# Attention values of two pairs of head groups: column tiles with a transpose by DMA in place of token-wise matmuls

## The chip, the cores and the metric

The kernel runs on one core of a Trainium2 chip. The metric is the device time of one execution in microseconds, lower is better; several executions are timed and the median is given. One further execution was recorded by the hardware profiler: its span runs from the first to the last instruction, and its own time, with what lies around the span, stands beside it in the table below.

## The reference: what is computed

Two layers follow each other twice: an attention with a compressive memory, and a feed-forward net with ReLU. The input has 2048 tokens of 640 features, all in bf16; there are 32 heads of 20 features, and the tokens are cut into 4 segments of 512.

```python
x = x + _A_ref(_layernorm(x), wq, wk, wv, wo, beta)
x = x + _B_ref(_layernorm(x), w1, w2)      # 640 -> 1728 -> 640
# ... and both once more

# _A_ref, for each segment s of 4 (q, k, v by head: [32, 512, 20])
logits = einsum('bhqd,bhkd->bhqk', qs, ks) * scale + mask   # causal in the segment
p      = softmax(logits)
a_dot  = einsum('bhqk,bhkd->bhqd', p, vs)
num    = einsum('bhld,bhde->bhle', phi(qs), M)
den    = einsum('bhld,bhd->bhl', phi(qs), z) + 1e-6
o      = g * num / den + (1 - g) * a_dot                    # g = sigmoid(beta)
M, z   = M + phi(ks)^T vs, z + sum(phi(ks))
# at the end: concat(o) @ wo
```

The change is about `a_dot`: the product of the softmax's numerators with the values, and the division by their sum.

## The kernel before

**A planner.** The kernel writes no fixed order. `plan` describes the work as some thirty streams (generators), each yielding operations (`Op`) with an engine, an assumed duration and what they wait for. `Sched.run` repeatedly takes the operation that can start first, with priorities (0 is the highest) as the tie-breaker, and so lays down each engine's order and its semaphore waits before anything runs. Slots (`Slot`, `Acq`) stand for buffers: PSUM banks, staging tiles, the padded queries and keys. Events (`S.set`, `Need`) link the streams. `dma` puts all transfers in this part of the program on SP's queue, which is worked off in order; `turn` (line 668) is a DMA that transposes 128x128 blocks, and the planner takes SP as held while it is under way.

The whole plan is made once for each price of a mode change of TensorE in `STARTS` (line 161), and the plan whose end in the planner's model, summed over four draws of random DMA delays (`late`), is the lowest is emitted (line 1534). TensorE is used in three modes, `full`, `rows` (scores: four row tiles, for four heads of 20 features) and `cols` (column tiles). An operation in `cols` is put off by up to `JOIN_NS` = 4 us if the array is in full mode, so that it can stand behind a set of scores. Where the planner sees TensorE idle for long, `keep_busy` puts in multiplications of the identity matrix that nothing uses (line 627).

**Attention.** The 32 heads form 8 groups of four. Two groups make a pair, and pairs are numbered by `m`: 0 to 3 for segment 0 of the first layer, 4 to 7 for segment 1, and so on to 31. For each pair:

- `scores` (line 1082) multiplies keys by queries, one set for each of five rounds; PSUM banks 0 and 1 (X) and 2 and 3 (Y) hold it.
- `exps` (line 1137) takes the exponential on ACT, 128x1024 elements at a time, into the buffer PT (two slots, one for each group of the pair); `causal` (line 1161) zeroes what lies above the diagonal on GpSimd.
- `apply` (line 1227) multiplies by the values, each of which has a 1 as its 21st element (`VAUG`), so that the row's sum comes out beside the product. When a group's matmuls are done, its PT slot is free for the next pair.

`apply` has two ways. *By tokens* (`values_by_token`, line 1181): PT is the stationary operand, 128 keys by 128 queries, and 21 columns of values are streamed, 40 matmuls for a group (4 heads x 10 blocks on or below the diagonal). The result has tokens on partitions, so DVE divides straight from PSUM into `o_sb` with three instructions for a group (lines 1209, 1210, 1213). *By column tiles* (lines 1236 to 1259): the values of one head, 21 to 32 columns wide, are the stationary operand in a quarter of the array, and PT is streamed, 16 matmuls for a group, the four heads of a block in four column tiles. The result has features on partitions. It is copied out of PSUM to `av` by DVE or ACT (`evac`, lines 1254 and 1255), both groups of the pair are transposed by one DMA to `avt` (`turn_av`, line 1263), and `divide` (line 1271) takes the reciprocal, multiplies by 1 - g, and writes `o_sb` with one instruction for each group (lines 1282, 1283, 1290). `av` and `avt` are single slots. The stream of `divide` has priority 6, that of `apply` 1, that of `turn_av` 2.

Pairs 0 to 3 (segment 0 of the first layer) go by tokens, pairs 4 to 31 by column tiles.

**Around it.** When all of a segment's `o_sb` is there, `turn_o` (line 1323) transposes it in two DMAs to `oT`, `out_proj` (line 1335) multiplies by wo, the result is added to x (line 1317), normalized (`ln_b`) and transposed again, and `ffn` follows. For segment 0 of the first layer these steps are marked as urgent (`HOT`). In the meantime TensorE does what lies ahead: queries, keys and values of the following segments (lines 640 and 643), and updates of the memory (line 1047). Queries and keys go to DRAM and come back in padded form (`spill` line 889, `fill` line 934), the latter's loads on SP's queue; phi(k) is transposed by a DMA (`turn_k`).

Of the kernel before, what the change touches and what calls it, by code (L numbers as in the profile page):

```python
# [14 lines left out]
NSEG = 4  # L15
# [4 lines left out]
G = H // 4  # L20
# [137 lines left out]

LONE_NS = 300.0
SWITCH_NS = 97.0  # L160
STARTS = [SWITCH_NS + 0.75 * (k - 32 // 2) for k in range(32)]
LATE_NS = 300.0
JOIN_NS = 4000.0
SEM_NS = 60.0
# [212 lines left out]
def pe(ns, fns, waits=(), acq=None, take=(), mode="full"):  # L377
    return Op([("pe", ns, fns, 190.0)], waits, acq=acq, take=take, mode=mode)
# [14 lines left out]
def evac(n, mode, vfn, afn, waits=(), psum=True):  # L393
    return Op([("act", (52.0 if psum else 94.0) + n / 1.2, [(afn, True)], 125.0),
               ("dve", 66.0 + n / (0.96 * mode), [(vfn, True)], 95.0)], waits, urgent=True)
# [12 lines left out]
def plan(switch, sb, sem_, psum, dram, A_x, A_wq, A_wk, A_wv, A_wo, A_beta, B_x, B_w1, B_w2, out):  # L408
# [435 lines left out]
    def vx(a, s):  # L844

        return 3 if (a, s) == (0, 0) else (NSEG * a + s) % 3
# [328 lines left out]
    def wide(g, hh):  # L1175

        return 32 if (g, hh) != (G - 1, 3) else DH + 1

    BY_TOKEN = ((0, 0),)

    def values_by_token(m, a, s, g0, vt):

# [37 lines left out]
    def done_values(a, s, g0, tk):  # L1220
        if g0 == G - 2:
            dmt = yield Need("dm", a, s)
            VA[vx(a, s)].release(tk, *dmt)
            if (a, s) == (0, 0):
                S.set("v00", tks=VA[3].tks)

    def apply(m):

        a, r = divmod(2 * m, NSEG * G)
        s, g0 = divmod(r, G)  # L1230
        vt = yield Need("v", a, s)
        if (a, s) in BY_TOKEN:
            tk = yield from values_by_token(m, a, s, g0, vt)
            yield from done_values(a, s, g0, tk)
            return
        sl = None
        ev = []
        for z in range(2):
            mk = yield Need("p", 2 * m + z)
            pt, mk = mk[0], mk[1:]  # L1240
            if sl is None:
                sl = yield Acq([AV])
            fns = []
            for j in range(NJ):
                for hh in range(4):
                    fns.append((lambda e, bk, j=j, hh=hh, pt=pt, g=g0 + z: e.matmul(  # L1246
                        bk.ap[32 * hh:32 * hh + wide(g, hh), 128 * j:L],
                        VAUG[vx(a, s)][:, j].rearrange("p h e -> p (h e)")[
                            :, (4 * g + hh) * (DH + 1):(4 * g + hh) * (DH + 1) + wide(g, hh)],
                        pt.ap[:, hh, PT_OFF[j]:PT_OFF[j] + L - 128 * j], start=(j == 0), stop=(j == NJ - 1)),  # L1250
                        j == NJ - 1 and hh == 3))
            bk, tk = yield pe(545.0, fns, mk + vt, acq=MISC, mode="cols")
            pt.release(tk)
            te = yield evac(L, 1, lambda e, sl=sl, z=z, bk=bk: e.tensor_copy(sl.ap[:, z], bk.ap),  # L1254
                            lambda e, sl=sl, z=z, bk=bk: e.activation(sl.ap[:, z], bk.ap, ACT.Copy), [tk] + sl.tks)
            bk.release(te)
            ev.append(te)
        S.set("av", m, tks=[sl] + ev)
        yield from done_values(a, s, g0, tk)

    LATER = range(len(BY_TOKEN) * G // 2, NSEG * G)

    def turn_av(m):
        ev = yield Need("av", m)
# [185 lines left out]
    def hot(f):  # L1450

        def g(a, s):
            if (a, s) not in HOT:
                yield from f(a, s)
                return
            gen = f(a, s)
            y = next(gen, None)
            while y is not None:
                if isinstance(y, Op):
                    y.urgent = 0.8  # L1460
                r = yield y
                try:
                    y = gen.send(r)
                except StopIteration:
                    return
        return g
# [5 lines left out]
    def each(f):  # L1472
        for a, s in AS:
            yield from f(a, s)

    def items(f, count):
        for n in (range(count) if isinstance(count, int) else count):
            yield from f(n)

    S.add(0, scores())  # L1480
    S.add(0, exps())
    S.add(5.5, items(causal, NSEG * G))
    S.add(1, items(apply, NSEG * G))
    S.add(2, items(turn_av, LATER))
    S.add(6, items(divide, LATER))
    S.add(2, each(hot(turn_o)))
# [31 lines left out]
def bass_interleave_layers__memory_aug_infini_attn__dense_activation_relu__prompt_kernel(  # L1518
    nc, A_x, A_wq, A_wk, A_wv, A_wo, A_beta, B_x, B_w1, B_w2, out,
):  # L1520
    with contextlib.ExitStack() as es:
        kept = {}

        def once(name, make):
            if name not in kept:
                kept[name] = make()
            return kept[name]

        sb = lambda name, shape, dtype=dt.bfloat16: once(name, lambda: es.enter_context(nc.sbuf_tensor(name, shape, dtype)))
        sem_ = lambda name: once("s_" + name, lambda: es.enter_context(nc.semaphore(name)))  # L1530
        psum = lambda name, shape: once(name, lambda: es.enter_context(nc.psum_tensor(name, shape, dt.float32)))
        dram = lambda name, shape: once(name, lambda: nc.dram_tensor(name, shape, dt.bfloat16, kind="Internal").ap())
        plans = [plan(k, sb, sem_, psum, dram, A_x, A_wq, A_wk, A_wv, A_wo, A_beta, B_x, B_w1, B_w2, out) for k in STARTS]
        S = min(plans, key=lambda p: sum(p.late(n) for n in range(4)))
        with nc.Block() as block:
            S.P.emit(block)
    return S
# [28 lines left out]
```

## Time and profile before

| what | value |
|---|---|
| three executions | 564.82, 566.28, 566.39 us |
| median | 566.28 us |
| profiled execution: time | 565.3 us |
| profiled execution: span | 563.5 us |
| matmuls by tokens (line 1197) | 320, that is 8 groups of 40 |
| matmuls by column tiles (line 1246) | 896, that is 56 groups of 16 |
| sets of 128x1024 exponentials (line 1155) | 320, mean 1022 ns |
| TensorE clock granted, mean | 1.000 |

A row of the profile's order of time gives the start and the length in microseconds, the engine (PE is TensorE, SPq the queue of SyncE), the line of the kernel, the operation, what it writes and reads, and how many like ones were merged; in square brackets stands the idle time of the engine just before, and what ended it. Matmuls are pipelined: the length of a row of several includes the drain of the last, so the time that a group holds the array is read from its start to the start of the next row. A row of the groups by line has the count, the busy time in us with the mean length of one in ns, and the idle time before them with what ended it. A row of the stages has, for each engine, its busy time and its number of instructions, then the granted clock, the DMA engines' busy share and GB/s.

### The profile page before, as it was taken

The page shows a single profiled execution, that of the slowest core. Times are in us where ns is not written, and L with a number is a line of the kernel's source. Part 1 is how long each engine was busy: PE and PEld are TensorE (multiplying, and loading weights), DVE is VectorE, ACT ScalarE, POOL GpSimd, SP SyncE. Part 2 cuts the span into 40 slices and gives each one's busy share as a digit, 9 for nine tenths or more (in the row PEclk, how much of TensorE's full clock was granted, in tenths as well). Part 3 has the DMA queues.
Part 4 walks back from the last instruction along what each step waited for, and adds up shares of the span by engine and source line. Part 5 has one row for each costly group of instructions (what it writes and reads, how often), then busy time and mean ns, then how long its engine had stood idle before and what let it go on. Part 6 is the DMA issues. An engine that isn't in the chain of part 4 may idle for free.

```text
span 563.5 us, 12875 instructions
## 1 busy us (share of the span) xinstructions
PE 556.4 (99%) x5219; PEld 305.0 (54%) x5219; DVE 420.1 (75%) x1070; ACT 404.2 (72%) x512; POOL 195.1 (35%) x302
## 2 busy tenths in 40 slices
PE   8999999999999999999999999999999999999998
PEld 7664555445554454645446544555445654665655
DVE  6989789888999689878898997688747964560202
ACT  4789998987788878778986688778878678113140
POOL 4544344333344335444433443035322433110000
PEclk9999999999999999999999999999999999999999
DMA  8695988383474136542375131880326410512101
GB/s 268 120 221 138 238 218 182 74 224 56 97 171 94 44 88 159 118 95 72 92 163 115 27 66 26 193 148 20 67 80 173 109 43 20 116 45 48 47 1 47
DMA packets 130109, 60.93 MB, mean 108 GB/s; under 512 B 108930, under 2 KB 119938, under 8 KB 130050
## 3 DMA queue, kind: packets, MB, share of 16 engines
q1 hardware_dynamic: 129830, 59.85, 45.5%
q8 instruction: 41, 0.67, 0.5%
q10 hardware_dynamic: 220, 0.26, 0.2%
q14 instruction: 18, 0.15, 0.1%
HBM read 20.57 MB, written 12.85 MB: 59 GB/s over the span
## 4 chain that ended last, share of the span: by engine, by line
PE 87%; DVE 8%; DMA 2%; ACT 1%; SPq 1%; issue 0%
PE ps L643 56%; PE ps L640 11%; PE ps L1103 8%; PE ps L1246 6%; DVE stats L651 2%; PE ps L996 2%; PE ps L1197 1%; PE ps L1047 1%; DVE x_sb L1317 1%; PE ps L1394 1%; DMA avt<-av 1%; DVE xn_tok L705 1%; SPq L913 1%; DMA oT<-o_sb 1%; ACT PT L1155 1%; DVE stg L816 1%
## 5 line engine op out<-in xcount | busy, mean ns | idle before, releaser
L1155 ACT ACTIVATE PT<-ps 128x1024 bf16<-128x1024 f32 x320 | 310.0, 1022 | 70.3 <-PE ps L1103 64.6
L1167 POOL TENSOR_SCALAR_AFFINE_SELECT PT<-PT 128x512 bf16<-128x512 bf16 x256 | 166.6, 668 | 268.2 <-ACT PT L1155 267.9
L643 PE MATMUL ps<-w_r,hT 128*128 128x320 bf16 (+2 forms) x768 | 123.0, 299 | 0.0
L643 PE MATMUL ps<-xnT,w_r 128*128 128x512 bf16 x416 | 113.3, 379 | 0.0
L1317 DVE TENSOR_TENSOR x_sb<-x_sb,ps 128x320 bf16<-128x320 bf16 (+1 forms) x128 | 60.3, 479 | 66.7 <-PE ps L643 66.0
L643 PEld LDWEIGHTS ps<-w_r,hT 128*128 128x128 bf16 x768 | 72.4, 98 | 31.9 <-issue 4.4
L1425 ACT ACTIVATE hT<-ps 128x512 bf16<-128x512 f32 x55 | 32.7, 598 | 50.0 <-PE ps L643 49.7
L1103 PE MATMUL ps<-pad 20*128 20x128 bf16 (+3 forms) x1024 | 64.8, 301 | 1.6 <-ACT PT L1155 0.9
L643 PEld LDWEIGHTS ps<-xnT,w_r 128*128 128x128 bf16 x416 | 39.7, 98 | 44.0 <-issue 3.2
L651 DVE BATCH_NORM_STATS2 stats<-x_sb 128x6 f32<-128x320 bf16 x126 | 56.4, 472 | 2.1 <-DMA x_sb<-in_A_x_dram 1.8
L1254 DVE CAST av<-ps 128x512 bf16<-128x512 f32 x53 | 36.2, 684 | 14.8 <-PE ps L1246 14.7
L1103 PEld LDWEIGHTS ps<-pad 20*128 20x128 bf16 x1024 | 18.3, 92 | 52.6 <-ACT PT L1155 25.6
L643 PE MATMUL ps<-wo_r,oT 128*128 128x320 bf16 x256 | 46.1, 299 | 0.0
L1246 PE MATMUL ps<-PT,v_aug 128*32 128x256 bf16 (+5 forms) x896 | 40.7, 302 | 0.0
L1423 DVE TENSOR_SCALAR hT<-ps 128x512 bf16<-128x512 f32 x49 | 33.4, 683 | 9.1 <-PE ps L643 9.0
L640 PE MATMUL ps<-xnT,w_r 128*128 128x512 bf16 x104 | 39.6, 380 | 0.0
L643 PE MATMUL ps<-wv_r,xnT 128*128 128x320 bf16 x192 | 36.7, 300 | 0.0
L643 PE MATMUL ps<-xnT,wk_r 128*128 128x512 bf16 (+1 forms) x140 | 36.1, 349 | 0.0
L643 PE MATMUL ps<-xnT,wq_r 128*128 128x512 bf16 (+1 forms) x140 | 34.9, 349 | 0.0
L665 POOL TENSOR_TENSOR rstd<-lnU,mhalf 128x2 f32<-128x2 f32 (+2 forms) x25 | 20.8, 831 | 38.0 <-DVE lnU L661 34.4
L816 DVE CAST stg<-ps 128x512 bf16<-128x512 f32 (+1 forms) x48 | 29.5, 618 | 3.3 <-PE ps L643 3.2
L1290 DVE TENSOR_TENSOR o_sb<-avt,rden 128x320 bf16<-128x320 bf16 x56 | 30.5, 562 | 0.6
(117 smaller groups left out, 695.8 us busy)
## 6 DMA issues: line engine op xcount, KB each, us to landing
pad<-scr SPq DMA_DIRECT2D x124, 80.0 KB
scr<-stg SPq DMA_DIRECT2D x34, 256.0 KB, 2.9
out_dram<-x_sb SPq DMA_DIRECT2D x15, 160.0 KB, 1.8
w_r<-in_B_w_dram SPq DMA_DIRECT2D x10, 216.0 KB, 4.2
w_r<-in_B_w_dram SPq DMA_DIRECT2D x13, 160.0 KB, 2.8
x_sb<-in_A_x_dram SPq DMA_DIRECT2D x9, 160.0 KB, 2.8
scr<-w_r SPq DMA_DIRECT2D x5, 256.0 KB, 3.6
x_sb<-in_A_x_dram SPq DMA_DIRECT2D x3, 320.0 KB, 7.2
```

What stands on the lines that cost most here:

```text
L640: bk, tk = yield pe(mm_ns(n), [(lambda e, bk, a=a, b=b: e.matmul(bk.ap[:, 0:n] if len(b.shape) == 2 else bk.ap[:, 0:n].rearrange("p (i n) ...
L643: tk = yield pe(mm_ns(n), [(lambda e, k=k, a=a, b=b, bk=bk: e.matmul(bk.ap[:, 0:n] if len(b.shape) == 2 else bk.ap[:, 0:n].rearrange("p (i ...
L651: tk = yield dve(320, 1, lambda e, c2=c2: e.bn_stats(stats6[:, t, c2, :], x_sb[:, t, c2 * 320:(c2 + 1) * 320]), xt)
L816: te = yield evac(N, 1, lambda e, sg=sg, bk=bk: e.tensor_copy(sg.ap[:, t0:t0 + N], bk.ap[:, 0:N]), lambda e, sg=sg, bk=bk: e.activation(sg ...
L1103: fns.append([(lambda e, z=z, j=j, hh=hh, N=N, o=o, sl=sl: e.matmul(ps[:, hh, o:o + N], sl.ap[32 * hh:32 * hh + DH, z, 0, 128 * j:128 * j ...
L1155: tx = yield act(1024, lambda e, dst=dst, src=src: e.activation(dst, src, ACT.Exp, scale=SCALE), sc + pw)
L1167: tm = yield pool(600.0, lambda e, reg=reg: e.affine_select(out=reg, in_=reg, pattern=[[0, 4], [1, 128]], compare_op=ALU.is_ge, fill=0.0, ...
L1246: fns.append((lambda e, bk, j=j, hh=hh, pt=pt, g=g0 + z: e.matmul(bk.ap[32 * hh:32 * hh + wide(g, hh), 128 * j:L], VAUG[vx(a, s)][:, j].re ...
L1254: te = yield evac(L, 1, lambda e, sl=sl, z=z, bk=bk: e.tensor_copy(sl.ap[:, z], bk.ap), lambda e, sl=sl, z=z, bk=bk: e.activation(sl.ap[:, ...
L1317: ta = yield dve(n, 1, lambda e: e.tensor_tensor(x_sb[:, t, c0:c0 + n], x_sb[:, t, c0:c0 + n], bk.ap[:, 0:n], ALU.add), [tk] + list(waits) ...
L1423: th = yield evac(512, 1, lambda e, dc=dc, bk=bk: e.tensor_scalar(hT[:, dc, :], bk.ap[:, :], 0.0, None, ALU.max), lambda e, dc=dc, bk=bk: ...
L1425: lambda e, dc=dc, bk=bk: e.activation(hT[:, dc, :], bk.ap[:, :], ACT.Relu), [tk] + HT.tks)
```

## The change

Three places change. The tuple `BY_TOKEN` held the (layer, segment) whose pairs go by tokens, segment 0 of the first layer and so pairs 0 to 3; it now holds the numbers of pairs, 2 and 3. Pairs 0 and 1 thereby go by column tiles, with the copy to `av`, the transpose to `avt` and `divide`; `LATER`, the list for which `turn_av` and `divide` run, now begins with them. And `STARTS` has 48 prices of a mode change, from 79.00 to 114.25 ns, where it had 32 from 85.00 to 108.25 with the same step; the old ones are all among the new.

```diff
-STARTS = [SWITCH_NS + 0.75 * (k - 32 // 2) for k in range(32)]
+STARTS = [SWITCH_NS + 0.75 * (k - 48 // 2) for k in range(48)]
...
-    BY_TOKEN = ((0, 0),)
+    BY_TOKEN = (2,3)
...
         vt = yield Need("v", a, s)
-        if (a, s) in BY_TOKEN:
+        if m in BY_TOKEN:
             tk = yield from values_by_token(m, a, s, g0, vt)
...
-    LATER = range(len(BY_TOKEN) * G // 2, NSEG * G)
+    LATER = [m for m in range(NSEG * G) if m not in BY_TOKEN]
```

## The prediction, made before the changed kernel was run

> **What bounds the kernel now.** I read the page's head first, then the busy time of each engine by stage, then the order of PE's instructions around the four groups that change.
>
> ```profile
> span 563.5 us, 12875 instructions
> PE 556.4 (99%) x5219; PEld 305.0 (54%) x5219; DVE 420.1 (75%) x1070; ACT 404.2 (72%) x512; POOL 195.1 (35%) x302
> ```
>
> ```profile
> core 0: us, PE busy (x) PEld busy (x) DVE busy (x) ACT busy (x) POOL busy (x), PEclk, DMA share, GB/s
> 20.00:80.00 60.00, 59.94 (x735) 34.51 (x733) 53.44 (x144) 55.31 (x74) 26.00 (x39) 1.00 0.82 198
> 80.00:84.00 4.00, 3.80 (x61) 2.34 (x60) 2.52 (x6) 3.98 (x6) 2.03 (x4) 1.00 1.24 213
> 84.00:110.00 26.00, 25.15 (x232) 13.07 (x232) 24.48 (x71) 22.83 (x29) 10.93 (x18) 1.00 0.62 140
> 110.00:500.00 390.00, 389.29 (x3640) 205.09 (x3640) 311.08 (x771) 296.75 (x359) 145.23 (x219) 1.00 0.43 98
> ```
>
> The reader is to see that PE is occupied almost throughout: it lacks 0.06 us of the 60 in the first segment's attention and 0.71 us of the 390 from 110 on. A microsecond of work taken from PE should therefore be a microsecond of time, unless the place it is taken from is one where PE would then have nothing else to do. All that the change touches lies between 20 and 80 us. So the question is what follows at 80.
>
> ```profile
> 80.34 1.40 PE L627 MATMUL ps<-ident 128*128 128x128 bf16 x22
> ...
> 82.00 0.51 PE L627 MATMUL ps<-ident 128*128 128x128 bf16 x6
> ...
> 84.00 0.31 PE L640 MATMUL ps<-wo_r,oT 128*128 128x320 bf16 x1 [0.21 <-DMA oT<-o_sb]
> 84.15 0.71 PE L643 MATMUL ps<-wo_r,oT 128*128 128x320 bf16 x4
> ```
>
> Line 627 multiplies the identity for nothing: the planner puts it where PE would stand still. 28 of them take 1.40 + 0.51 = 1.9 us, and 0.21 us more is plain idle. So of the 4 us from 80 to 84 PE has no useful work for some 2.1 us, though it counts as busy for most of them: all work ahead has been used up, and it waits for the transposed attention output of segment 0. That output is late for this reason:
>
> ```profile
> 76.84 0.65 PE ps L1197 x22
> ...
> 80.10 3.86 DMA oT<-o_sb
> ```
>
> ```profile
> 78.66 0.48 DVE L1213 TENSOR_TENSOR o_sb<-ps,rden 128x320 bf16<-128x320 f32 x1
> ```
>
> ```profile
> 77.35 2.71 SPq L671 DMA_TRANSPOSE phk<-phs  x1
> ```
>
> The last values of pair 3 end at about 77.5, DVE finishes them at 79.14, SP is held by another transpose until 80.06, and the two transposes land at 83.96. Pair 3 itself comes when its exponentials come, and these follow a loop:
>
> ```profile
> 19.30 0.40 PE L1103 MATMUL ps<-pad 20*128 20x512 bf16 x4 [0.62 <-DMA pad<-stg]
> ...
> 72.77 0.39 PE L1103 MATMUL ps<-pad 20*128 20x384 bf16 x6
> ```
>
> ```profile
> 42.00 1.94 ACT L1155 ACTIVATE PT<-ps 128x1024 bf16<-128x1024 f32 x2 [0.35 <-PE ps L1103]
> 44.83 1.94 ACT L1155 ACTIVATE PT<-ps 128x1024 bf16<-128x1024 f32 x2 [0.89 <-PE ps L1103]
> ```
>
> Scores fill the PSUM halves X and Y, ACT needs 1.94 us for both, and only then can the next scores start: 42.00 to 44.83 is 2.83 us, of which ACT stands 0.89. From the first round at 19.30 to the twentieth at 72.77 the mean is 53.47 / 19 = 2.81 us. The loop thus runs at its round trip (two exponentials, two hand-overs and one set of scores), and PE's other work hardly lengthens it. The moment of 84 us is set by this loop and by what follows it, not by how much PE has to do before.
>
> **The change part by part.** Pairs 0 and 1 are four head groups. *Removed*, and *added* on PE:
>
> ```profile
> 42.42 1.16 PE L1197 MATMUL ps<-w_r,PT 128*128 128x21 bf16 x40
> 43.44 0.38 PE L640 MATMUL ps<-hT,wk_r 128*128 128x512 bf16 x1
> ...
> 91.87 0.31 PE L643 MATMUL ps<-wv_r,xnT 128*128 128x320 bf16 x1
> 92.11 0.73 PE L1246 MATMUL ps<-PT,v_aug 128*32 128x512 bf16 x16
> 92.77 0.45 PE L643 MATMUL ps<-wv_r,xnT 128*128 128x320 bf16 x2
> ...
> 97.40 0.73 PE L1246 MATMUL ps<-PT,v_aug 128*32 128x512 bf16 x16
> 98.06 0.34 PE L996 MATMUL ps<-BD,w_r 128*128 128x84 bf16 x3
> ```
>
> A group by tokens holds PE for 43.44 - 42.42 = 1.02 us; sixteen matmuls in column tiles hold it for 92.77 - 92.11 = 98.06 - 97.40 = 0.66 us. Saved: 0.36 us. Where column tiles follow full-array work and not scores, entering costs more: 92.11 - 91.87 = 0.24 us behind a 320-column matmul, against 84.15 - 84.00 = 0.15 without a change of mode, so 0.09 us. Four groups save between 4 x 0.27 = 1.1 and 4 x 0.36 = 1.4 us. I take 1.4, since the planner waits up to 4 us to put such a group behind scores.
>
> Elementwise work and the transpose:
>
> ```profile
> L1254 DVE CAST av<-ps 128x512 bf16<-128x512 f32 x53 | 36.2, 684 | 14.8 <-PE ps L1246 14.7
> L1290 DVE TENSOR_TENSOR o_sb<-avt,rden 128x320 bf16<-128x320 bf16 x56 | 30.5, 562 | 0.6
> L1282 DVE RECIPROCAL rden<-avt 128x32 f32<-128x32 bf16 x28 | 9.6, 342 | 6.7 <-DMA avt<-av 6.7
> L1283 DVE TENSOR_TENSOR rden<-rden,omg 128x32 f32<-128x32 f32 x28 | 8.3, 296 | 0.5
> L1213 DVE TENSOR_TENSOR o_sb<-ps,rden 128x320 bf16<-128x320 f32 x8 | 3.9, 485 | 0.1
> L1210 DVE TENSOR_TENSOR rden<-rden,omg 128x16 f32<-128x16 f32 x8 | 2.2, 270 | 0.1
> L1209 DVE RECIPROCAL rden<-ps 128x16 f32<-128x16 f32 x8 | 2.0, 250 | 1.0 <-PE ps L1197 1.0
> ```
>
> ```profile
> L1255 ACT ACTIVATE av<-ps 128x512 bf16<-128x512 f32 x3 | 1.8, 597 | 3.3 <-PE ps L1246 3.3
> ```
>
> A pair by tokens costs DVE 2 x (250 + 270 + 485) = 2.01 us. In column tiles it costs 2 x 684 for the copies out of PSUM, 342 + 296, and 2 x 562: 3.13 us. Two pairs add 2.2 us to DVE, or, if ACT copies, take 0.5 us from DVE and add 4 x 597 = 2.4 us to ACT. From 20 to 80 DVE has 6.6 us free and ACT 4.7, so either fits as a sum. Whether it fits in place is open: on the loop's path it costs between nothing (the copy falls into one of the 0.89 us waits, or on DVE) and 2.4 us (all four on ACT and each ahead of a ready exponential). I take 0.3, near the lower end, since 53 of the 56 copies of this kind run on DVE.
>
> ```profile
> L671 SPq DMA_TRANSPOSE avt<-av x28: 1231/1240/1911, 95.4 to 484.8; - x28
> ...
>   PEld ps L640: 2.2, 7
> ...
> DMA to landing us min/median/max: 2.7/2.8/4.5
> ```
>
> Two transposes of 256 KB are added, each 1.24 us of SP and 2.8 us to landing, 4.5 at worst. Queued behind them on SP are the fills of the padded queries and keys (line 934), the spills (889) and loads:
>
> ```profile
> 41.15 2.25 SPq L532 DMA_DIRECT2D wo_r<-in_A_wo_dram  x2
> 45.88 0.33 SPq L528 DMA_DIRECT2D x_sb<-in_A_x_dram  x1
> ```
>
> SP issues nothing between 43.40 and 45.88, so the first transpose finds room; without that room it would put a fill off by 1.2 us each, 2.5 in all. I take nothing. The division of pair 1 hides behind some 30 us: the pair's values begin at 42.42, and its output is needed with pair 3's at 79.14. A copy waiting on DVE also holds the casts behind it, which free PSUM for PE: 2.2 us in 56 groups, so 0.2 us for four.
>
> *The sum.* Saved on PE 1.4 us; but since the loop sets the 84 us, PE reaches its end of useful work 1.4 us sooner and the planner fills 1.4 us more with line 627 or idles. What comes after 84 keeps its work. So the end moves by 0.3 (loop) and 0.1 (half of the held casts), less what the planner regains of the 0.92 us that the output waits for SP (79.14 to 80.06), of which I take 0.7: -0.3. The profiled execution has 563.5 us of span and took 565.3 us; the median of the three runs is 566.28, 1.0 higher. Of the profiled execution the sum makes 565.0; set against the median, the forecast is 566.0.
>
> **The planner.** Everything from the first issue on is planned anew, for 48 prices of a mode change (79.00 to 114.25 ns) where there were 32 (85.00 to 108.25), all of the old ones among them; the plan with the least late end in its own model is emitted. The order may thus change anywhere, and this bounds how well any sum can do.
>
> **The rivals.**
>
> *Gain kept.* If the output of segment 0 lands earlier because SP is free at once (0.92 us) and pair 3 isn't cut by scores, the 2.1 us without work at 80 to 84 shrink and the 1.4 us count: 566.3 - 1.4 - 0.9 = 564.0, and 566.3 - 1.4 - 2.1 = 562.8 at best. For it speaks that PE lacks almost nothing after 110. Against it, the loop's 2.81 us.
>
> *Loop delayed: slower.* Column-tile values may be held for scores for up to 4 us, and they release the exponentials' buffer PT only then. That wait is seen in the profile, on ACT:
>
> ```profile
>   ACT PT L1155: 4.4, 3
> ```
>
> Three of 56 such groups (line 1246) stopped an exponential, 1.5 us each; no group by tokens is named there. If one group of each pair does so, the loop is 2.9 us later, and PE, with its work ahead used up, starves that much longer at 80: 566.3 + 2.9 = 569.2. With all copies on ACT (2.4) it is 571.6. It decides from the point where the delays exceed what DVE and SP lose after 77.5, about 1.6 us. [...]
>
> *Unlucky order: slower.* From 110 to 500 the present plan leaves PE only 0.71 us of gaps; a new one can lose 1 to 4 us at a segment's change, as this one loses 0.85 from 84 to 110 and 2.1 ahead of it: 568 to 570. Against it: the choice is made by the same measure, from more plans.
>
> **How the numbers follow.** No change to speak of 0.34, gain kept 0.29, loop delayed 0.22, unlucky order 0.15. Of the first, 0.02 spill over on either side; of the last, 0.01 each may turn out within the bound or faster. This gives faster 0.32, within 0.31, slower 0.37, where the bound is 0.3% of 566.28, or 1.7 us, about what a measurement of this kernel can tell from no change. The forecast's own range is 564.6 to 568.0. The range for 8 in 10 goes from 562.4 (all of the gain, and half of the 0.85) to 570.6 (loop delayed, with half of the copies on ACT: 569.2 + 1.2, and 0.2 for held casts).
>
> **What would show it.** Right, if four groups of line 1246 stand ahead of 50 us at 0.66 us each, line 627 between 78 and 84 grows from 28 towards 50 matmuls, and the first matmul on oT stays within a microsecond of 84.0. The gain is kept if that matmul comes before 83 and line 627 doesn't grow. The loop is delayed if the twentieth set of scores comes after 74 and ACT's exponentials name line 1246 before 80. The forecast is wrong in its reason if the difference arises after 110, by gaps of PE that this profile doesn't have.

## The result, and the profile after

The changed kernel takes 569.70 us (569.30 to 570.25) against 566.07 (564.82 to 566.39): a ratio of 1.0069, with an interval from 1.0051 to 1.0087. That is 3.6 us slower, and more than a measurement of this kernel is uncertain. The profiled execution took 570.25 us with a span of 568.5.

The head of the page and the stages of the changed kernel, with the columns of the same views before the change:

```profile
span 568.5 us, 12669 instructions
PE 557.2 (98%) x5119; PEld 302.6 (53%) x5120; DVE 416.7 (73%) x1064; ACT 408.3 (72%) x518; POOL 194.2 (34%) x302
```

```profile
20.00:80.00 60.00, 58.07 (x647) 32.89 (x646) 52.62 (x140) 53.42 (x70) 23.53 (x36) 0.97 0.82 196
80.00:84.00 4.00, 3.67 (x31) 1.29 (x29) 3.93 (x15) 3.78 (x5) 2.66 (x4) 1.00 0.47 108
84.00:110.00 26.00, 25.27 (x251) 13.61 (x251) 24.62 (x71) 23.30 (x32) 11.10 (x17) 1.00 0.99 200
110.00:500.00 390.00, 386.67 (x3615) 200.80 (x3607) 303.73 (x754) 302.32 (x365) 145.85 (x223) 1.00 0.45 95
```

PE now lacks 60 - 58.07 = 1.93 us in the stage where the change lies, against 0.06 before, and 390 - 386.67 = 3.33 us from 110 on, against 0.71. The second difference, 2.6 us, lies where the kernel's work was not changed at all.

The order of time of PE around the four groups and up to the output of segment 0:

```profile
32.95 0.73 PE L1246 MATMUL ps<-PT,w_r 128*32 128x512 bf16 x16
33.61 0.40 PE L1103 MATMUL ps<-pad 20*128 20x512 bf16 x4
...
50.83 0.73 PE L1246 MATMUL ps<-PT,w_r 128*32 128x512 bf16 x16
51.49 0.39 PE L640 MATMUL ps<-hT,wq_r 128*128 128x512 bf16 x1
...
53.54 0.90 PE L627 MATMUL ps<-ident 128*128 128x128 bf16 x13
54.70 0.68 PE L627 MATMUL ps<-ident 128*128 128x128 bf16 x9
...
57.12 0.45 PE L640 MATMUL ps<-wv_r,hT 128*128 128x320 bf16 x1 [1.43 <-DMA hT<-xn_tok]
...
74.66 0.39 PE L1103 MATMUL ps<-pad 20*128 20x384 bf16 x6
...
85.61 0.31 PE L640 MATMUL ps<-wo_r,oT 128*128 128x320 bf16 x1 [0.15 <-DMA oT<-o_sb]
```

The four groups stand at 32.95, 39.49, 45.64 and 50.83 us and hold PE for 0.66 us each, as computed. The multiplications of the identity that stood between 80 and 84 are gone; 24 stand between 53.0 and 55.3 now (22 of them in the two rows shown), and behind them PE idles 1.43 us for a transposed activation. The twentieth set of scores starts at 74.66 instead of 72.77, the first matmul on oT at 85.61 instead of 84.00. Where the loop of scores and exponentials loses this time is seen in ACT's order of time, here of the changed kernel, with the scores from PE's between the two rows:

```profile
51.11 5.78 ACT L1155 ACTIVATE PT<-ps 128x1024 bf16<-128x1024 f32 x6
...
59.63 0.61 PE L1103 MATMUL ps<-pad 20*128 20x384 bf16 x8
...
60.28 2.96 ACT L1155 ACTIVATE PT<-ps 128x1024 bf16<-128x1024 f32 x3 [2.37 <-PE ps L1103]
```

The 28th exponential starts at 55.84 us, 0.5 earlier than before the change (56.36), the 29th at 60.28, 3.0 later (57.28). ACT stood 2.37 us for scores that on PE have their place behind the wait for the activation. So it is this wait, with slow matmuls at a granted clock of 0.50 behind it (last section), and not the four copies, that sets the loop back for good; DVE made these copies (ACT's first copy of this kind starts at 415.9 us).

Then the stalls after 170 us, in the same view of PE; the kernel before has none of them (its waits from 110 on are 0.44 us at 166.41 and 0.23 at 195.96):

```profile
179.90 0.31 PE L640 MATMUL ps<-wv_r,xnT 128*128 128x320 bf16 x1 [1.35 <-DMA xnT<-xn_tok]
...
291.76 0.38 PE L1047 MATMUL ps<-v_aug,phk 128*128 128x147 bf16 x3 [0.29 <-DMA phk<-phs]
...
300.69 0.40 PE L1103 MATMUL ps<-pad 20*128 20x512 bf16 x4 [0.32 <-ACT PT L1155]
...
331.45 0.39 PE L640 MATMUL ps<-xnT,w_r 128*128 128x512 bf16 x1 [0.40 <-DVE v_aug L867]
...
359.58 0.40 PE L1103 MATMUL ps<-pad 20*128 20x512 bf16 x4 [0.34 <-DMA pad<-scr]
...
372.97 0.34 PE L996 MATMUL ps<-BD,stg 128*128 128x84 bf16 x3 [0.35 <-DVE om_sb L1007]
```

They add up to 1.35 + 0.29 + 0.32 + 0.40 + 0.34 + 0.35 = 3.05 us and have six different reasons in places that the change doesn't touch. Ahead of the largest, no multiplication of the identity was planned, as the planner does where it expects PE to stand for long (from 300 ns on, `IDLE_NS`). It probably reckoned with an earlier landing of these transposes; its planned times are not shown here:

```profile
174.83 2.94 SPq L671 DMA_TRANSPOSE xnT<-xn_tok  x2
```

These two transposes held SP's queue for 2.94 us and landed at 179.85.

To see where the time arises, I gave each matmul of the traces a fixed weight (0.42 ns for each column, as 320 columns take 0.13 us from 61.01 on; at least 25 ns, as the 40 by tokens hold PE for 1.02 us; a quarter of it, an estimate, for those of four tiles at once: four scores of 512 columns, 0.22 us by this weight, hold PE for 0.33 us from 33.61 on, mode changes included; none for the identity) and summed what was still to be done at one and the same time. The table shows by how many us a kernel is behind the one before (negative: ahead). At 0 it shows the work that the kernel has less. e2, e5 and e8 are kernels of the next section. A few matmul records are missing in a trace (the page above has 5119 matmuls; it counts 5120 weight loads), so differences of half a microsecond mean nothing.

```
us    after    e2    e5    e8
  0    -2.1  -0.2  -0.2  -2.1
 60     2.9   2.2   0.9   0.7
 80     2.9   2.5   1.5   0.3
100    -0.1  -1.1  -1.7  -2.6
170     0.1  -0.3   1.1   0.3
200     1.3   0.3   2.2  -0.1
300     1.7   0.5   2.7  -0.4
400     4.5   3.7   4.9   1.3
560     4.7   5.4   5.6   0.6
```

The changed kernel falls behind between 50 and 60, has regained it by 100, and is level with the kernel before until 170. Most of its lasting loss comes between 170 and 200, where the longest wait stands, and between 300 and 400. The waits listed explain part of it: from 300 to 400 they come to 1.4 us, the loss in the table to 2.8.

### The profile page after: what moved, and what is told of

It is laid out like the page before. It is cut to its first block, busy times and chain, and to the rows that moved or that the text cites. A ratio compares the mean times of both kernels' runs of the same rounds, so it can differ in the third digit from the quotient of the medians.

```text
span 568.5 us, 12669 instructions
## 1 busy us (share of the span) xinstructions
PE 557.2 (98%) x5119; PEld 302.6 (53%) x5120; DVE 416.7 (73%) x1064; ACT 408.3 (72%) x518; POOL 194.2 (34%) x302
## 4 chain that ended last, share of the span: by engine, by line
PE 73%; DVE 16%; DMA 7%; ACT 2%; issue 1%; SPq 1%; POOL 0%; DVEq 0%
PE ps L643 48%; PE ps L640 9%; PE ps L1103 7%; PE ps L1246 5%; DVE stats L651 3%; DMA xnT<-xn_tok 2%; ACT PT L1155 2%; DVE x_sb L1317 1%; PE ps L996 1%; DVE xn_tok L693 1%; DMA phk<-phs 1%; PE ps L1047 1%; DVE o_sb L1290 1%; DVE phs L964 1%; DMA avt<-av 1%; DVE stg L816 1%
## 5 line engine op out<-in xcount | busy, mean ns | idle before, releaser
L643 PE MATMUL ps<-w_r,hT 128*128 128x320 bf16 (+2 forms) x768 | 124.4, 299 | 0.1
L1317 DVE TENSOR_TENSOR x_sb<-x_sb,ps 128x320 bf16<-128x320 bf16 (+1 forms) x128 | 60.5, 479 | 67.8 <-PE ps L643 67.4
L1425 ACT ACTIVATE hT<-ps 128x512 bf16<-128x512 f32 x57 | 34.1, 599 | 46.3 <-PE ps L643 46.0
L1103 PE MATMUL ps<-pad 20*128 20x512 bf16 (+3 forms) x1024 | 64.7, 302 | 1.7 <-ACT PT L1155 0.7
L1254 DVE CAST av<-ps 128x512 bf16<-128x512 f32 x57 | 38.9, 683 | 18.6 <-PE ps L1246 18.4
L1423 DVE TENSOR_SCALAR hT<-ps 128x512 bf16<-128x512 f32 x47 | 32.0, 682 | 8.6 <-PE ps L643 8.3
L816 DVE CAST stg<-ps 128x512 bf16<-128x512 f32 (+1 forms) x45 | 27.6, 616 | 14.2 <-PE ps L643 14.1
L1290 DVE TENSOR_TENSOR o_sb<-avt,rden 128x320 bf16<-128x320 bf16 x60 | 33.5, 579 | 0.5
```

What stands on the lines that cost most here:

```text
L643: tk = yield pe(mm_ns(n), [(lambda e, k=k, a=a, b=b, bk=bk: e.matmul(bk.ap[:, 0:n] if len(b.shape) == 2 else bk.ap[:, 0:n].rearrange("p (i ...
L816: te = yield evac(N, 1, lambda e, sg=sg, bk=bk: e.tensor_copy(sg.ap[:, t0:t0 + N], bk.ap[:, 0:N]), lambda e, sg=sg, bk=bk: e.activation(sg ...
L1103: fns.append([(lambda e, z=z, j=j, hh=hh, N=N, o=o, sl=sl: e.matmul(ps[:, hh, o:o + N], sl.ap[32 * hh:32 * hh + DH, z, 0, 128 * j:128 * j ...
L1290: to = yield dve(320, 1, lambda e, dst=dst, src=src, rz=rz: e.tensor_tensor(dst, src, rz, ALU.mult), [tg] + OSB.tks)
L1317: ta = yield dve(n, 1, lambda e: e.tensor_tensor(x_sb[:, t, c0:c0 + n], x_sb[:, t, c0:c0 + n], bk.ap[:, 0:n], ALU.add), [tk] + list(waits) ...
L1425: lambda e, dc=dc, bk=bk: e.activation(hT[:, dc, :], bk.ap[:, :], ACT.Relu), [tk] + HT.tks)
```

## The experiments

Two theories were put against each other. *The work*: the column tiles of pairs 0 and 1, with their copies and transposes, cost the time. *The plan*: the new constants only made the planner lay out all of the program anew, and the new order is worse than the old one for reasons that have little to do with the four groups. A third, *the queue*, is a part of the first: the two added transposes push back other DMAs on SP.

### Work and order crossed (e1, e2)

To separate the two I recorded the order that the planner had made for one kernel and had it lay down the other kernel's operations in that order, the new ones at the place of those that they replace. e1 has the old order (made at the price of 85.75 ns) and the new work, e2 the new order (89.50 ns) and the old work. The functions added for this shift the lines by about 50.

```diff
-STARTS = [SWITCH_NS + 0.75 * (k - 48 // 2) for k in range(48)]
+PRICE = 85.75                                     # e2: 89.5
+TURN_NS, DIV_NS = (0, 2000), (6000, 6000)         # e2: (0, 0), (7000, 7000)
+PLANNED, EMITTED = (0, 1, 2, 3), (2, 3)           # e2: (2, 3), (0, 1, 2, 3)
...
+        first = plan(PRICE, *args, BY_TOKEN=PLANNED)
+        S = plan(PRICE, *args, BY_TOKEN=EMITTED, ranks=ranks)
```

> The order of the kernel before is kept operation by operation on every engine; only pairs 0 and 1 go by column tiles, put where their token-wise groups stood, with the two transposes where SP was free or nearly so. Theory 'order' (the four groups cost next to nothing themselves; the time was lost because the planner, planning anew, emitted an order with more stalls, most of them after 170 us): 566 us, within 1.7 of the kernel before. Theory 'direct' (the copies, divisions and transposes of these two pairs delay segment 0): 569 to 571 us, as the changed kernel.

> The order of the changed kernel is kept operation by operation; only pairs 0 and 1 go back to tokens. Theory 'order': 569 to 571 us, as the changed kernel, since its stalls after 170 us remain. Theory 'direct': 566 us, as before.

Measured: e2 570.34 us (570.13 to 572.08), ratio 1.0077 [1.0060, 1.0095]. With pairs 0 and 1 back to tokens, the new order is as slow as with column tiles (569.70). Taking the four groups out thus doesn't bring the time back, and PE waits late in e2 at places where it waits in the changed kernel (there at 300.69, 331.45 and 372.97, for 0.32, 0.40 and 0.35 us):

```profile
298.87 0.40 PE L1154 MATMUL ps<-pad 20*128 20x512 bf16 x4 [0.32 <-ACT PT L1206]
...
329.63 0.39 PE L691 MATMUL ps<-xnT,w_r 128*128 128x512 bf16 x1 [0.40 <-DVE v_aug L918]
...
372.18 0.34 PE L1047 MATMUL ps<-BD,stg 128*128 128x84 bf16 x3 [0.35 <-DVE om_sb L1058]
```

These waits belong to the order, not to the column tiles. What e2 can't tell is how much it loses because its tokens stand in an order that was made for other work; that the column tiles don't need to cost 3.6 us is shown by e8 and e18 below. e1 was not the clean opposite: 572.40 us (570.13 to 575.78), ratio 1.0112 [1.0065, 1.0159]. In the old order the new work costs 6 us (4 to 9 by the interval). The queue of SP in e1 shows one reason:

```profile
38.38 3.09 SPq L722 DMA_TRANSPOSE avt<-av  x1
...
42.14 1.50 SPq L985 DMA_DIRECT2D pad<-scr  x4
...
54.35 1.31 SPq L722 DMA_TRANSPOSE avt<-av  x1
55.70 1.69 SPq L722 DMA_TRANSPOSE hT<-xn_tok  x1
```

The first added transpose held SP for 3.09 us and put the fill of the next pair's padded queries and keys off from 39.67 (before) to 42.14; the second put the transposed activation off from 53.46 to 55.70. So of the four combinations of work and order three are slow, and only the old work in the old order is fast.

### The same work, other plans (e3, e4, e5)

If the plan is a draw, then the unchanged kernel must be able to lose as much by a change that leaves its work alone. The price of a mode change is such a thing: it only steers the planner. e3 is the kernel before at the price that the changed kernel chose, e4 the changed kernel at the price that the kernel before chose, e5 the kernel before with the list of 48 prices.

```diff
-STARTS = [SWITCH_NS + 0.75 * (k - 32 // 2) for k in range(32)]
+STARTS = [89.5]                                                     # e3, on the kernel before
+STARTS = [85.75]                                                    # e4, on the changed kernel
+STARTS = [SWITCH_NS + 0.75 * (k - 48 // 2) for k in range(48)]      # e5, on the kernel before
```

> The kernel before, planned for the one price of a mode change that the changed kernel's planner picks (89.50 ns in place of its own 85.75). Theory 'order': the time of a plan is largely a draw, so this may lie anywhere from 564 to 575 us, and 2 us or more from 566. Theory 'direct': tokens make the difference whatever the plan, so 566, within 1.5.

> The changed kernel, planned for the price that the kernel before picks (85.75 ns in place of 89.50). Theory 'order': 564 to 575 us, not tied to 569.7. Theory 'direct': 569.7, within 1.5.

> Only the 48 prices in place of 32; pairs 0 to 3 by tokens as before. The planner now picks 114.25 ns, a new plan of unchanged work. Theory 'draw' (what the chip makes of a plan is largely chance, and the kernel before is one of the good draws): 568 to 573 us, though no operation was changed. Theory 'direct' (column tiles in pairs 0 and 1 cost the time): 566, within 1.7.

Measured: e3 576.53 us, ratio 1.0180 [1.0165, 1.0195]; e4 570.29, 1.0069 [1.0052, 1.0085]; e5 572.49, 1.0099 [1.0070, 1.0128]. The kernel before loses 10.3 us by another price alone, though by one that its planner would not have picked. And the half of the change that touches no work, the longer list, costs 6.5 us by the medians when it is made alone (4.0 to 7.2 by the interval): the planner then picks the price 114.25, whose plan it takes for the best. (In the changed kernel the list does nothing: 89.50 is among the old 32.) The stage from 110 to 500 of e2 and of e5 shows a loss like the changed kernel's:

```profile
110.00:500.00 390.00, 384.85 (x3584) 199.60 (x3583) 301.26 (x751) 301.69 (x365) 145.80 (x221) 1.00 0.44 94
```

```profile
110.00:500.00 390.00, 385.64 (x3608) 200.93 (x3607) 300.02 (x748) 301.77 (x367) 146.85 (x223) 1.00 0.43 97
```

PE lacks 5.15 us there in e2 and 4.36 in e5, against 3.33 in the changed kernel and 0.71 in the kernel before.

### How wide the draw is (e6 to e12, e16 to e18)

The next kernels have one price each, like e3 and e4, for either kind of work: `STARTS = [p]` and nothing else. e11's price, 80.50, is the one that is best in the planner's model when the random DMA delays in `late` are drawn up to 1000 ns instead of 300, a choice meant to be robust.

> The kernel before, planned for 85.00 ns, the price its planner ranks next. Theory 'draw': anywhere from 566 to 576 us, more likely above 568. Theory 'direct': 566, within 1.7.

> The changed kernel, planned for 83.50 ns, the price its planner ranks second. Theory 'draw': anywhere from 565 to 574 us, above and below 569.7. Theory 'direct': 569.7, within 1.7.

> The changed kernel, planned for 82.00 ns, the price its planner ranks third. Theory 'draw': anywhere from 565 to 574 us, and not the same as at 83.50. Theory 'direct': 569.7, within 1.7.

> The changed kernel, planned for 85.00 ns, to be set against the kernel before at the same price (567.8 us). Theory 'draw': 565 to 575 us, with no fixed distance. Theory 'direct': 3.6 us above it, 571.4.

> The changed kernel, planned for 114.25 ns, to be set against the kernel before at the same price (572.5 us). Theory 'draw': 565 to 576 us. Theory 'direct': 576.1.

> The changed kernel, planned for 80.50 ns, the price that its planner would pick if it reckoned with random DMA delays of 1000 ns instead of 300. Theory 'draw': 565 to 574 us. If such a choice finds sturdier plans, it is at the lower end and beats both kernels: 563 to 566.

> The kernel before, planned for 82.00 ns, to be set against the changed kernel at the same price (566.6 us). Theory 'draw': 566 to 577 us, with no fixed distance. Theory 'direct': 563.0.

> The changed kernel, planned for 91.00 ns, which its planner ranks fourth. Theory 'draw': 565 to 574 us; below 565.5 it would beat both kernels. Theory 'direct': 569.7, within 1.7.

> The kernel before, planned for 91.00 ns, a sixth pair of plans with the same price. Theory 'draw': 566 to 577 us, on either side of e16. Theory 'direct': 3.6 us below e16.

> The changed kernel, planned for 95.50 ns, which its planner ranks fifth. Theory 'draw': 565 to 574 us; below 565.5 it would beat both kernels. Theory 'direct': 569.7, within 1.7.

All plans of both kinds, in us; "planner" is the mean end of the four draws in the planner's own model, which is no time of the chip but what it chooses by:

```
price ns   work before: measured, planner    work after: measured, planner
 80.50                                       569.57 (e11)     563.7
 82.00     570.90 (e12)     570.6            566.56 (e8)      562.8
 83.50                                       567.61 (e7)      562.5
 85.00     567.79 (e6)      565.2            568.49 (e9)      566.5
 85.75     566.07 (before)  564.8            570.29 (e4)      568.1
 89.50     576.53 (e3)      572.2            569.70 (after)   561.7
 91.00     571.82 (e17)     569.6            569.94 (e16)     562.9
 95.50                                       566.66 (e18)     563.3
114.25     572.49 (e5)      564.6            571.37 (e10)     569.9
```

Three readings. First, identical work takes from 566.1 to 576.5 us by the plan alone, and the changed work from 566.6 to 571.4. Not all of this is chance: e3, e12 and e17 are plans that the planner itself puts 4.8 to 7.4 us behind that of the kernel before. But the three plans of the old work that it puts within 0.6 us of each other (114.25, 85.75, 85.00) take 572.5, 566.1 and 567.8 us on the chip. Second, at the same price the changed work is slower by 4.2 us once (85.75) and by 0.7 once (85.00), and faster by 6.8, 4.3, 1.9 and 1.1 in the four others; the mean is -1.5 us with a standard error of 1.6, not to be told from nothing. In five of these six the planner's model has the difference with the same sign. The plans of one kind are not all independent draws, either: e16 waits at 300.09, 331.02, 359.31 and 372.70 us almost as the changed kernel does. No plan of the changed work that was run beats the kernel before, though the five that the planner ranks first of the 48 are among them (89.50, 83.50, 82.00, 91.00, 95.50): e8 has a ratio of 1.0005 [0.9986, 1.0025], e18 1.0014 [1.0001, 1.0026]. Third, the planner's choice takes its model's errors along. Where it chose the best of 48, the chip took 7.9 us longer than the model (e5) and 8.0 us longer (after), the two largest differences of the table; for the plan of the kernel before it is 1.3. Its model puts the changed kernel's plan 3.1 us ahead of that of the kernel before (561.7 and 564.8), and the chip puts it 3.6 behind. The robust choice, e11, didn't help.

The stage of e8 from 110 on shows that the changed work can be laid out almost without gaps:

```profile
110.00:500.00 390.00, 388.80 (x3641) 203.73 (x3639) 304.32 (x762) 298.86 (x361) 148.09 (x221) 1.00 0.43 98
```

PE lacks 1.20 us there, at 566.56 us in all. The gaps alone don't order the plans, though. The same stage of e12:

```profile
110.00:500.00 390.00, 388.57 (x3676) 204.81 (x3673) 297.15 (x757) 298.93 (x357) 144.62 (x222) 1.00 0.44 96
```

It lacks only 1.43 us and takes 570.90. Most of its loss lies where PE counts as busy: in the multiplications of the identity. The same stage for line 627 alone, which has columns for PE and its weight loads only, in the kernel before and in e12:

```profile
110.00:500.00 390.00, 1.11 (x11) 0.79 (x11) 1.00 0.43 98
110.00:500.00 390.00, 6.87 (x102) 6.00 (x102) 1.00 0.44 96
```

That is 5.8 us more, and e12's span is 569.0 - 563.5 = 5.5 us longer. In e3 they take 9.01 us, in e4 6.08, in e17 5.62, in e9 4.97. So there are two ways in which a plan is slow. Where the planner foresees that PE will stand, it fills the time with line 627 and ranks the plan low, as it does these. Where it doesn't foresee it, PE waits and the plan looks good: line 627 takes only 0.99 us in the changed kernel and 1.58 in e5, and both lose by waits. A choice by the model can keep out the first kind alone.

### What the new work costs in the old order (e13, e14, e15)

e1 left open why the new work is slow in the old order. e13 issues the added transposes 3 and 4 us later, behind the fills; e14 puts only pair 0 on column tiles, e15 only pair 1 (with its transpose as late as in e13).

```diff
-TURN_NS, DIV_NS = (0, 2000), (6000, 6000)
-PLANNED, EMITTED = (0, 1, 2, 3), (2, 3)
+TURN_NS, DIV_NS = (3000, 6000), (6000, 6000)      # e13
+PLANNED, EMITTED = (0, 1, 2, 3), (1, 2, 3)        # e14
+PLANNED, EMITTED = (0, 1, 2, 3), (0, 2, 3)        # e15, with TURN_NS = (0, 6000)
```

> As e1 (the old order, pairs 0 and 1 by column tiles), but on SP the first of the two added transposes now stands behind the fill of the padded queries and keys, and the second behind both transposes of segment 2's normalized input, which e1 put it between. Theory 'queue' (e1 lost its time because the added transposes pushed that fill and the second input transpose 2 us later each): 566 to 568 us, TensorE not idle for hT near 60 us. Theory 'copies' (the added copies and divisions on DVE cost it): 570 to 572, as e1.

> The old order, only pair 0 by column tiles, its transpose ahead of the fill as in e1. Theory 'queue': the delayed fill alone, 567 to 569 us. Theory 'copies': half of e1's loss, 568 to 569, with the loss after 40 us of the copies' kind (waits ended by DVE). If neither pair costs much alone: 566.

> The old order, only pair 1 by column tiles, its transpose behind both transposes of segment 2's input. Theory 'queue': 566, within 1.5, since nothing urgent stands behind it. Theory 'copies': 568 to 569.

Measured: e13 570.96 us (568.96 to 572.14), ratio 1.0063 [1.0043, 1.0084]; e14 568.63, 1.0036 [1.0015, 1.0057]; e15 567.91, 1.0016 [0.9993, 1.0039], which can't be told from no change. *The queue* is only partly right: e13's median is 1.4 us below e1's (their intervals overlap), and most of the loss stays. The order of time of PE in e13:

```profile
65.42 0.98 PE L1098 MATMUL ps<-v_aug,phk 128*128 128x147 bf16 x12 [1.12 <-DMA phk<-phs]
...
75.11 0.39 PE L1154 MATMUL ps<-pad 20*128 20x384 bf16 x6
...
87.10 0.31 PE L691 MATMUL ps<-wo_r,oT 128*128 128x320 bf16 x1 [0.41 <-DMA oT<-o_sb]
```

The wait for the transposed activation, 1.14 us at 60.34 in e1, is gone, but now the transposed phi(k) is late (1.12 us), and the twentieth set of scores comes 2.3 us later than before, the output of segment 0 3.1 us later. ACT's order of time in e13 shows a reason for part of it:

```profile
41.80 1.94 ACT L1206 ACTIVATE PT<-ps 128x1024 bf16<-128x1024 f32 x2 [0.35 <-PE ps L1154]
45.27 0.60 ACT L1305 ACTIVATE av<-ps 128x512 bf16<-128x512 f32 x1 [1.53 <-DMA avt<-av]
45.77 1.94 ACT L1206 ACTIVATE PT<-ps 128x1024 bf16<-128x1024 f32 x2
```

`av` is a single slot. With pair 0's transpose issued later, the copy of pair 1 out of PSUM found the slot taken, stood on ACT for 1.53 us, and the exponentials queued behind it began at 45.77 instead of 44.83, although those of the round before had begun at 41.80 instead of 42.00. So one copy on ACT set the loop back by 1.1 us. Most of the rest comes at the wait for phi(k): the scores at 62.53 are 1.06 us later than before (61.47), those at 66.68, which on PE stand behind that wait, 2.34 us (64.34). On SP the second added transpose, at 58.55, now stands directly ahead of that of phi(k), which is issued at 59.91 instead of 57.57. So an early transpose pushed the fill here (2.5 us in e1), a late one the exponentials (1.1 us in e13) and the next transpose (2.3). Why e14 with only one transpose also loses 2.3 us, stays open.

## Why the prediction was wrong

The time, 569.70, lies in the range, but the forecast of no change, 566.0 (up to 568.0 in its own range), was wrong, and the sign that the prediction named for a wrong reason is what happened: the lasting difference arises after 110, with 2.6 us more of gaps on PE, which the profile before doesn't have. That the range holds the time is no merit of the sum: its upper end, 570.6, was worked out for a delayed loop, which is not what made the loss. Its chances were nearer than its forecast: slower had 0.37, the most of the three.

- *The failed step* is the part on the planner. It said that a new order "bounds how well any sum can do", gave it 0.15, and argued against it that "the choice is made by the same measure, from more plans". This took the measure for a measurement. The plans with the best ends in the model were 7.9 and 8.0 us worse on the chip than in it. Whoever takes the best of many by a model favours plans whose waits the model overlooks. For the changed work, the five plans that it ranks first took 3.4 to 8.0 us longer than it said, the three that it put at 566.5 to 569.9 only 1.5 to 2.2. That there were more plans did not matter in the changed kernel (its price is among the old 32); in e5 it did. The weight should have been larger: the same step with unchanged work, e5, gives 572.5 us, and the plan that ranks next, e6, 567.8; the other three plans of unchanged work are slower, too (570.9, 571.8, 576.5), though these the planner ranks low itself. The row for it was on the table: a plan in which PE lacks 0.71 us of 390 leaves little room for a better one. The size that the rival gave, 568 to 570, fits; it put the loss at a segment's change, and the runs show waits scattered over the run.
- *Four groups at 0.66 us instead of 1.02*: right, at all four places (the last at 50.83 us, not ahead of 50).
- *The loop sets the 84 us*: right in kind. The scores came 1.9 us later and oT 1.6 us later. But the 0.3 was a term for copies on the loop's path, and the copies are not what delayed it: in the changed kernel the loop was 1.1 us behind at 40.27, but 0.5 ahead at the 28th exponential, and all of the delay that stayed comes at the wait for the activation at 57.12. Part of it is the lower clock behind that wait (0.50 for 3.4 us), which only the profiled one of the four executions shows (last section). The prediction had no term for scores that stand behind another wait on PE. A copy on the loop's path is seen in e13, at 1.1 us; that the 2.4 of the prediction is near the 2.3 of e13 is chance.
- *The added transposes, "I take nothing"*: wrong in the old order. The free stretch of SP from 43.40 to 45.88 was not the place of the first: pair 0's values end by 37 us, and e1 issued it at 38.38, ahead of a fill. There it held SP for 3.09 us instead of 1.24 and shifted the fill by 2.5 us, the second shifted an activation by 2.2; the prediction's price without room on SP was 2.5 in all. In the changed kernel they took 1.25 and 1.35 us of SP (at 41.32 and 58.17); that they are why PE idled 1.43 us for an activation at 57.12 is not shown.
- *The loop delayed, rival*: both of its signs are there (the twentieth scores after 74, and an exponential at 40.27 that waited 0.40 us for line 1246), but it is not what decides. What line 1246 held up was made good by the 28th exponential. By 100 us the changed kernel had regained its whole delay: between 80 and 84, where PE had no useful work for 2.1 us before, it now had some.
- *Line 627 growing towards 50 between 78 and 84*: wrong. None is left there; 24 stand at 53 to 55 us, where work now ran out first.
- *Gain kept*: not seen in the changed kernel. In e8 its sign is there: no line 627 between 78 and 84, and the first matmul on oT comes 2.3 us earlier than before,

```profile
81.69 0.31 PE L640 MATMUL ps<-wo_r,oT 128*128 128x320 bf16 x1
```

  and at 100 us e8 is 2.6 us ahead. By 170 it is level again, and it takes 566.56 us. So the step of the rival that fails there is that the gain lasts; whether the changed work gains something in the mean over plans (-1.5 us, with an error as large) stays open.

## What to carry to other kernels

Where a planner, a search or a scheduler lays out the whole program from a model, every edit draws a new program, and the present one is a lucky draw if it was kept for being fast: here identical work spread over 10 us, over 6 among plans that the model held to be equally good, while the prediction put the edit's own saving of PE time at 1.4. Compare such edits over several plans of both kinds, and choose the plan to keep by measured times: the model sorts out plans whose idle time it foresees, but not those with waits that it doesn't. Within a fixed order, a transpose added to SP's queue cost its place in it (2.5 and 2.2 us for what stood behind the two in e1), and the single buffer that it held until it landed cost 1.53 us on ACT in e13: look up both before adding one.

## What the runs showed of the hardware

After the idle 1.43 us at 57 us, the profiled execution of the changed kernel shows a lower granted clock in its stages of ten us, and half the clock from 57.1 to 60.5:

```profile
50.00:60.00 10.00, 8.57 (x121) 4.74 (x119) 7.69 (x17) 7.51 (x10) 4.50 (x7) 0.85 0.82 181
60.00:70.00 10.00, 10.00 (x123) 6.03 (x115) 9.71 (x29) 9.36 (x13) 3.18 (x5) 0.98 0.85 236
...
57.10:60.50 3.40, 3.38 (x55) 2.25 (x56) 1.26 (x6) 1.03 (x3) 0.48 (x1) 0.50 1.01 214
```

In the order of time the matmuls of 320 columns start 0.24 us after each other until 60.42 and 0.13 at 61.01:

```profile
57.12 0.45 PE L640 MATMUL ps<-wv_r,hT 128*128 128x320 bf16 x1 [1.43 <-DMA hT<-xn_tok]
57.36 1.27 PE L643 MATMUL ps<-wv_r,hT 128*128 128x320 bf16 x4
58.43 1.27 PE L1197 MATMUL ps<-w_r,PT 128*128 128x21 bf16 x40
59.63 0.61 PE L1103 MATMUL ps<-pad 20*128 20x384 bf16 x8
60.18 0.45 PE L640 MATMUL ps<-wv_r,hT 128*128 128x320 bf16 x1
60.42 0.75 PE L643 MATMUL ps<-wv_r,hT 128*128 128x320 bf16 x4
61.01 0.30 PE L640 MATMUL ps<-wv_r,hT 128*128 128x320 bf16 x1
61.14 0.71 PE L643 MATMUL ps<-wv_r,hT 128*128 128x320 bf16 x4
...
62.10 0.31 PE L640 MATMUL ps<-wv_r,hT 128*128 128x320 bf16 x1
62.25 0.71 PE L643 MATMUL ps<-wv_r,hT 128*128 128x320 bf16 x4
62.79 0.38 PE L640 MATMUL ps<-hT,wk_r 128*128 128x512 bf16 x1
...
64.34 1.16 PE L1197 MATMUL ps<-w_r,PT 128*128 128x21 bf16 x40
65.35 0.30 PE L640 MATMUL ps<-wv_r,hT 128*128 128x320 bf16 x1
...
66.55 0.40 PE L1103 MATMUL ps<-pad 20*128 20x384 bf16 x8
66.88 0.31 PE L640 MATMUL ps<-wv_r,hT 128*128 128x320 bf16 x1
```

So the granted clock was 0.50 for some 3.4 us. From start to start, five matmuls of 320 columns took 1.31 us at 57.12 and 0.83 at 60.18, against 0.69 at 62.10; the 40 by tokens took 1.20 at 58.43 against 1.01 at 64.34, and the scores at 59.63 took 0.55 against 0.33 at 66.55. That is some 1.2 us more in all. e16, whose plan is much the same up to there, with 1.47 us of idle time at the same place, shows such a dip, too: 0.89 and 0.94 in the same two stages, and 0.24 us from the start of the matmul of 320 columns at 59.57 to the next. e14, with 1.40 us at 54.73, shows none (1.00 in its stage from 20 to 80). That the gap brought the dip on is not shown: the wait of 1.35 us at 179.90 in the same execution of the changed kernel has none behind it (1.00 from 180 to 190). The three other timed executions of the changed kernel show a mean clock of 1.000 and spans of 567.6 to 568.1, so the dip belongs to the profiled one (568.5, mean clock 0.997). Without it the median is 569.59 us instead of 569.70, so the dip makes 0.1 of the 3.6 us.
